# Five GpSimd DRAIN instructions among the last output scatters of a recurrence-and-experts kernel

## The chip, the core and the metric

The kernel runs on one core of one Trainium2 chip. The metric is device time in microseconds, from an execution's start to its end; several executions are timed and the median is taken. A separate, profiled execution left the page and the trace from which the rows below come. In those rows PE is TensorE (matmuls; PEld its weight loads), DVE is VectorE, ACT is ScalarE, POOL is GpSimd, SP is SyncE, and a small q behind a name (POOLq) means the engine's sequencer, which waits, branches and issues.

## What is computed

A gated recurrence over 4 sequences of 5056 steps, then a layer of 8 experts of which each token uses one. Cut to what matters:

```python
f = lower_bound + (1 - lower_bound) * sigmoid(f_logit)      # (4, 5056, 256)
h[t] = f[t] * h[t-1] + (1 - f[t]) * x[t]                    # per sequence; y[t] = h[t]
logits = y @ w_gate                                          # 20224 tokens, 8 experts
e = argmax(logits); p = softmax(logits)[e]
out[token] = p * (relu(y[token] @ w1[e]) @ w2[e])            # 256 -> 1024 -> 256
```

## The kernel before

**Units and buckets.** The 20224 tokens are cut into 79 units of 256. Each unit is gated, scanned, split into two fp16 halves and routed. Its rows are then written by GpSimd into a bucket of their expert in device memory: one indirect DMA of 128 rows at a time, the scatters to `buckets` (line 399, in `place`).

**Expert steps.** A step takes 256 rows of buckets (one tile of 256 or two of 128). `fetch` lets SP load them transposed into `xT` (line 531), with their gate weights and token numbers in `me` (line 533). `gemm1` makes the hidden layer in four pieces that ACT (line 567) and DVE (line 547) write into `hT`. `gemm2` multiplies `hT` with `w2s` on PE (lines 598 to 600), for the two halves of 128 tokens in turn. ACT scales each half into `ob` (line 604, three buffers in turn), and GpSimd writes it with an indirect DMA to the rows of `out` (line 605): the output scatters, two to a step. `step` runs `gemm1` of one step and `gemm2` of the step before it.

**Order.** In the main loop units run beside steps, their pieces placed by `fill`. PE, ACT and DVE keep the order in which the code is written; GpSimd and SP are ordered by the scheduler from the dependencies. GpSimd's queue holds nothing but scatters there: 158 to `buckets` and 162 to `out`. When the units are done, the loop at the end of the function runs what is left, with nothing beside it:

```python
    while todo or fetched:
        step(lambda k: None)
    while pend:
        gemm2(*factors(*pend.pop(0)), lambda k: None)
```

It makes 20 turns, and the last `gemm2` follows them: 21 pairs of output scatters in all, one pair to a turn and one behind. Up to three further tiles (`MAYBE`) are run behind a branch (lines 878 to 883) if the data asks for them; in this data it doesn't, and GpSimd then executes an `INC_SWDGE_SEM` instruction in the other arm (line 880), which sets the counts that the scatters of that arm would have set.

**The end.** At the close of the program (all of it recorded under line 967) SP waits for what is still open, every engine executes a DRAIN, a barrier joins them, GpSimd clears the semaphores, and a second barrier ends the program. GpSimd has one DRAIN at the start of the program too (line 963), and none between.

Of the kernel before, what the change touches and what calls it, by code (L numbers as in the profile page):

```python
# [45 lines left out]
INLINE = mybir.DependencyInfo(mybir.DependencyClass.NoSync, mybir.DependencyReason.SCHED_ONLY)  # L46
# [19 lines left out]
def moe_kernel(ctx: ExitStack, tc: tile.TileContext, x, fl, lb, wg, w1, w2, cst, tok, out, xb, S):  # L66
    nc = tc.nc
# [160 lines left out]
    scatters, based, pace = [], {}, []  # L228
# [3 lines left out]
    def inline(d, kind):  # L232

        for n in lined["O" if kind == "S" else "S"]:
            tc.add_manual_dep(d.ins, n, INLINE, reason="in the order of the row")
        lined["O" if kind == "S" else "S"].clear()
        lined[kind].append(d.ins.name)

    def free(d, *groups, keep=()):

        for k in groups:
            tc.declare_no_dep(d.ins, group=k, keep=[s.ins for s in keep], reason="different rows")
# [120 lines left out]
    def place(g, i0, ng, rows, m, sh, ex, oh, mx):  # L363
# [34 lines left out]
        def scatter(i):  # L398
            d = nc.gpsimd.indirect_dma_start(  # L399
                out=xb[:, :], out_offset=bass.IndirectOffsetOnAxis(ap=idx[:, i:i + 1], axis=0),  # L400
                in_=rows[:, i, 0:ROW], in_offset=None)
            free(d, "scatter", "load")
            if (i0 + ng) * P + P <= CAP:

                free(d, "blank")
            if pace:
                tc.add_manual_dep(d.ins, pace[0], PACED, reason="scatters apart")
            tc.add_to_no_dep_group("scatter", d.ins)
            inline(d, "S")
            scatters.append(d)  # L410
# [127 lines left out]
    def bases(t, tiles):  # L538

        if t not in based:  # L540
            based[t] = [nc.tensor.value_load(i[1], min_val=0, max_val=(E - 1) * WE) for _, i in tiles]
        return based[t]
# [6 lines left out]
    def gemm1(t, tiles, xT, me, n, fill):  # L549
        hT = p2.tile([P, 2, NF, UNIT], F16, tag="hT", name=f"hT{t}")  # L550
        evs = bases(t, tiles)
        for b in range(NF // 2):
            ps = pg1.tile([P, 2, UNIT], F32, tag="g1", name=f"g1_{t}_{b}")
            for q in range(2):
                f = 2 * b + q
                a = 0
                for ev, (nt, _) in zip(evs, tiles):
                    for c in range(2):
                        hi = w1s[:, ds(ev + (c * F + f * P), P)]
                        lo = w1s[:, ds(ev + (2 * F + c * F + f * P), P)]  # L560
                        o = ps[:, q, a:a + nt]
                        nc.tensor.matmul(o, lhsT=hi, rhs=xT[:, c, a:a + nt], start=c == 0, stop=False)  # L562
                        nc.tensor.matmul(o, lhsT=hi, rhs=xT[:, 2 + c, a:a + nt], start=False, stop=False)  # L563
                        nc.tensor.matmul(o, lhsT=lo, rhs=xT[:, c, a:a + nt], start=False, stop=c == 1)  # L564
                    a += nt
            hh = hT[:, 0, 2 * b:2 * b + 2, :n]
            pace[:] = [nc.scalar.activation(hh, ps[:, :, :n], AF.Relu).ins.name]  # L567
            behind()
            owed.append((hT[:, 1, 2 * b:2 * b + 2, :n], ps[:, :, :n], hh))
            drip(DRIP)  # L570
            fill(b)
        behind()
        return t, n, [ev for ev, (nt, _) in zip(evs, tiles) for _ in range(nt // P)], hT, me, tiles

    def factors(t, n, evs, hT, me, tiles):
        fac = sm.tile([P, 2], F32, tag="fac", name=f"fac{t}", bufs=3)
        ti, a = [], 0
        for nt, (_, _, ei, skip, _) in tiles:
            j = slice(a // P, (a + nt) // P)
            nc.scalar.activation(fac[:, j], me[:, j, 0], AF.Copy, scale=ei)  # L580
            to = me.bitcast(I32)[:, j, 1:2]
            if skip is not None:
                at = sm.tile([P, 1], I32, tag="ti", name=f"ti{t}_{a}", bufs=4)
                nc.vector.tensor_scalar(at, to[:, 0, :], skip, None, op0=ALU.add)
                to = at.unsqueeze(1)
            ti += [to[:, k, :] for k in range(nt // P)]
            a += nt
        return t, evs, hT, fac, ti

    def gemm2(t, evs, hT, fac, ti, fill):  # L590
        for j, ev in enumerate(evs):
            po = pg2.tile([P, 512], F32, tag="g2", name=f"g2_{t}_{j}")
            for f in range(NF):
                hi = w2s[:, ds(ev + f * D, D)]
                lo = w2s[:, ds(ev + (2 * F + f * D), D)]
                hh = hT[:, 0, f, j * P:(j + 1) * P]
                hl = hT[:, 1, f, j * P:(j + 1) * P]
                nc.tensor.matmul(po[:, :D], lhsT=hh, rhs=hi, start=f == 0, stop=False)  # L598
                nc.tensor.matmul(po[:, :D], lhsT=hh, rhs=lo, start=False, stop=False)  # L599
                nc.tensor.matmul(po[:, :D], lhsT=hl, rhs=hi, start=False, stop=f == NF - 1)  # L600
                if f == NF // 2 - 1:
                    fill(4 + 2 * j)
            ob = p2.tile([P, D], F32, tag="ob", name=f"ob{t}_{j}", bufs=3)
            pace[:] = [nc.scalar.activation(ob, po[:, :D], AF.Copy, scale=fac[:, j:j + 1]).ins.name]  # L604
            d = nc.gpsimd.indirect_dma_start(  # L605
                out=out[:, :], out_offset=bass.IndirectOffsetOnAxis(ap=ti[j], axis=0),
                in_=ob, in_offset=None, bounds_check=N - 1, oob_is_err=False)
            free(d, "out")
            tc.add_to_no_dep_group("out", d.ins)
            inline(d, "O")  # L610
            fill(5 + 2 * j)


    plan, n, taken = [], 0, 0
# [23 lines left out]
    todo, placing, drips, total, held = [], [], [], [], []  # L638
# [31 lines left out]
    def release(n=1):  # L670

        while n and held:
            held.pop(0)()
            n -= 1
# [47 lines left out]
    queue, fetched, pend, nst = [], [], [], 0  # L722

    def ready():
        return sum(t for t, _ in todo) + sum(f[4] for f in fetched)

    def prefetch():
        nonlocal nst
        while todo and len(fetched) < 3:
            tiles = [todo.pop(0)]  # L730
            if tiles[0][0] == P and todo and todo[0][0] == P:
                tiles.append(todo.pop(0))
            fetched.append(fetch(nst, tiles))
            nst += 1

    def step(fill, second=True):

        prefetch()
        if len(pend) > 1:
            gemm2(*factors(*pend.pop(0)), lambda k: None)  # L740
        last = factors(*pend.pop(0)) if pend and second else None
        pend.append(gemm1(*fetched.pop(0), fill))
        prefetch()

        def then(k):
            if k == 5 and fetched:
                bases(*fetched[0][:2])
            fill(k)
        if last:
            gemm2(*last, then)  # L750
        else:
            for k in range(4, 8):
                fill(k)
# [32 lines left out]
    for w in ORDER.split():  # L786
        k, n = w[0], int(w[1:] or 0)
# [53 lines left out]
    def fill(k):  # L841
        nonlocal here
        while coming and coming[0][0] <= here:
            coming.pop(0)[1]()
        here += 1
        short = ready() < SHORT
        if short or k in (1, 3) or k == 0 and len(held) > 4 or k == 5 and len(held) > 8:
            release(1 + short)
# [20 lines left out]
    spare = []  # L869
    while len(spare) < MAYBE and todo:  # L870
        spare.insert(0, todo.pop())
    while todo or fetched:
        step(lambda k: None)
    while pend:
        gemm2(*factors(*pend.pop(0)), lambda k: None)

    if spare:
        n = nc.values_load(total[0])
# [93 lines left out]
```

## Time and profile before

| | |
|---|---|
| median of 3 runs | 1018.64 us (1015.17 to 1020.44) |
| the profiled execution's own time | 1019.52 us |
| its span, first to last instruction | 1017.6 us |
| PE busy | 931.3 us (92%) |
| POOL busy | 330.2 us (32%), 326 instructions |
| mean granted TensorE clock | 0.987 of full |
| last matmul, last scatter, end | about 1004, 1005.6, 1017.6 us |

The page gives busy time by engine over the whole span. Waits, DRAINs and barriers are the sequencers' and not counted as busy there, so the closing sequence shows on the page only as an empty last slice; its instructions come out when the trace is asked for their line.

### The profile page before, as it was taken

The page shows a single profiled execution, that of the slowest core. Times are in us where ns is not written, and L with a number is a line of the kernel's source. Part 1 is how long each engine was busy: PE and PEld are TensorE (multiplying, and loading weights), DVE is VectorE, ACT ScalarE, POOL GpSimd, SP SyncE. Part 2 cuts the span into 40 slices and gives each one's busy share as a digit, 9 for nine tenths or more (in the row PEclk, how much of TensorE's full clock was granted, in tenths as well). Part 3 has the DMA queues.
Part 4 walks back from the last instruction along what each step waited for, and adds up shares of the span by engine and source line. Part 5 has one row for each costly group of instructions (what it writes and reads, how often), then busy time and mean ns, then how long its engine had stood idle before and what let it go on. Part 6 is the DMA issues. An engine that isn't in the chain of part 4 may idle for free.

```text
span 1017.6 us, 29588 instructions
## 1 busy us (share of the span) xinstructions
PE 931.3 (92%) x10971; PEld 850.5 (84%) x10971; DVE 656.9 (65%) x1816; ACT 499.4 (49%) x971; POOL 330.2 (32%) x326
## 2 busy tenths in 40 slices
PE   3538879999997999999999999999999999999994
PEld 2426779999986999998988999888888888899994
DVE  7898879887866787777878777676644322223220
ACT  4566545555555555555565555564433333333331
POOL 0151143433433334444443443334333111121111
PEclk9998999999999999999999999999999999999997
DMA  7997678778786887899998677775423222221210
GB/s 256 340 340 194 131 158 169 156 157 162 158 159 154 162 175 151 169 178 191 193 200 172 157 174 153 149 167 126 103 77 78 49 53 53 51 51 41 48 45 19
DMA packets 239774, 145.54 MB, mean 143 GB/s; under 512 B 205966, under 2 KB 207248, under 8 KB 237585
## 3 DMA queue, kind: packets, MB, share of 16 engines
q1 hardware_dynamic: 224272, 102.02, 47.5%
q0 software_dynamic: 15360, 41.60, 14.4%
q8 instruction: 94, 1.54, 0.7%
q14 instruction: 48, 0.39, 0.1%
HBM read 58.57 MB, written 43.16 MB: 100 GB/s over the span
## 4 chain that ended last, share of the span: by engine, by line
PE 72%; DVE 10%; DMA 8%; issue 3%; ACT 3%; SPq 2%; POOL 1%; POOLq 0%; ACTq 0%; DVEq 0%
PE g L562 12%; PE g L564 12%; PE g L563 12%; PE g L598 11%; PE g L599 11%; PE g L600 11%; DMA w2s<-in_w 3%; DMA ft<-in_f 3%; DVE xt L305 2%; DMA xT<-buckets 2%; DVE hT L547 2%; DVE ft L330 1%; PE wps L178 1%; PE tp L339 1%; SPq L531 1%
## 5 line engine op out<-in xcount | busy, mean ns | idle before, releaser
L562 PE MATMUL g<-xT,w1s 128*128 128x128 f16 (+1 forms) x1968 | 401.7, 237 | 11.5 <-DMA xT<-buckets 5.5
L564 PE MATMUL g<-xT,w1s 128*128 128x128 f16 (+1 forms) x1968 | 401.8, 237 | 0.0
L563 PE MATMUL g<-xT,w1s 128*128 128x128 f16 (+1 forms) x1968 | 401.8, 237 | 0.0
L598 PE MATMUL g<-w2s,hT 128*128 x1296 | 353.5, 273 | 3.8 <-DVE am L308 2.1
L600 PE MATMUL g<-w2s,hT 128*128 x1296 | 353.5, 273 | 0.0
L599 PE MATMUL g<-w2s,hT 128*128 x1296 | 353.4, 273 | 0.0
L547 DVE SCALAR_TENSOR_TENSOR hT<-g,hT 128x512 f16<-128x512 f32 x324 | 220.4, 686 | 205.0 <-ACT hT L567 202.8
L567 ACT ACTIVATE hT<-g 128x512 f16<-128x512 f32 x324 | 190.8, 593 | 128.9 <-PE g L564 123.3
L605 POOL DMA_INDIRECT out_dram<-ob,me x142 | 143.7, 1012 | 333.9 <-ACT ob L604 258.4
L399 POOL DMA_INDIRECT buckets<-rows,idx x158 | 166.3, 1053 | 259.6 <-ACT hT L567 162.5
L563 PEld LDWEIGHTS <-w1s 128*128 x1968 | 193.5, 98 | 17.5 <-issue 10.4
L562 PEld LDWEIGHTS <-w1s 128*128 x1968 | 193.4, 98 | 10.3 <-DMA xT<-buckets 1.5
L564 PEld LDWEIGHTS <-w1s 128*128 x1968 | 193.5, 98 | 7.1
L604 ACT ACTIVATE ob<-g,fac 128x256 f32<-128x256 f32 x162 | 76.3, 471 | 197.3 <-PE g L600 189.4
L599 PEld LDWEIGHTS <-hT 128*128 128x128 f16 x1296 | 126.8, 98 | 16.6 <-issue 2.9
L598 PEld LDWEIGHTS <-hT 128*128 128x128 f16 x1296 | 126.8, 98 | 16.4 <-issue 2.5
L600 PEld LDWEIGHTS <-hT 128*128 128x128 f16 x1296 | 126.8, 98 | 14.9
L305 DVE TENSOR_TENSOR_SCAN xt<-ft,xt,xt 128x256 f32<-128x256 f32 (+2 forms) x156 | 110.7, 728 | 0.0
L278 ACT ACTIVATE ft<-ft,fa,fs 128x256 f32<-128x256 f32 x158 | 91.1, 591 | 0.8
L330 DVE SCALAR_TENSOR_TENSOR ft<-xt,m,ft 128x256 f16<-128x256 f32 x158 | 72.6, 480 | 28.9 <-ACT ft L323 24.5
L323 ACT ACTIVATE ft<-xt,m 128x512 f16<-128x512 f32 x79 | 57.0, 721 | 69.5 <-DVE m L320 67.8
L274 ACT ACTIVATE ft<-ft 128x512 f32<-128x512 f32 x79 | 49.2, 622 | 64.7 <-DMA ft<-in_f 54.5
(128 smaller groups left out, 609.9 us busy)
## 6 DMA issues: line engine op xcount, KB each, us to landing
ft<-in_f SPq DMA_DIRECT2D x79, 256.0 KB
xt<-in_x SPq DMA_DIRECT2D x79, 256.0 KB
w2s<-in_w SPq DMA_DIRECT2D x14, 1024.0 KB
rows<-ft SPq DMA_TRANSPOSE x158
buckets<-rows,idx POOLq DMA_INDIRECT x158
out_dram<-ob,me POOLq DMA_INDIRECT x142
ws<-in_w SPq DMA_DIRECT2D x2, 1024.0 KB
xT<-buckets SPq DMA_TRANSPOSE x126
```

The source lines that it names most:

```text
L278: nc.scalar.activation(ft[:, c, :], ft[:, c, :], AF.Identity, scale=fs[:, c:c + 1], bias=fa[:, c:c + 1])
L305: nc.vector.tensor_tensor_scan(xt[:, c, a:b], ft[:, c, a:b], xt[:, c, a:b], ini, op0=ALU.mult, op1=ALU.subtract)
L399: d = nc.gpsimd.indirect_dma_start(out=xb[:, :], out_offset=bass.IndirectOffsetOnAxis(ap=idx[:, i:i + 1], axis=0), in_=rows[:, i, 0:ROW], ...
L547: nc.vector.scalar_tensor_tensor(lo, ps, 0.0, hh, op0=ALU.max, op1=ALU.subtract)
L562: nc.tensor.matmul(o, lhsT=hi, rhs=xT[:, c, a:a + nt], start=c == 0, stop=False)
L563: nc.tensor.matmul(o, lhsT=hi, rhs=xT[:, 2 + c, a:a + nt], start=False, stop=False)
L564: nc.tensor.matmul(o, lhsT=lo, rhs=xT[:, c, a:a + nt], start=False, stop=c == 1)
L567: pace[:] = [nc.scalar.activation(hh, ps[:, :, :n], AF.Relu).ins.name]
L598: nc.tensor.matmul(po[:, :D], lhsT=hh, rhs=hi, start=f == 0, stop=False)
L599: nc.tensor.matmul(po[:, :D], lhsT=hh, rhs=lo, start=False, stop=False)
L600: nc.tensor.matmul(po[:, :D], lhsT=hl, rhs=hi, start=False, stop=f == NF - 1)
L605: d = nc.gpsimd.indirect_dma_start(out=out[:, :], out_offset=bass.IndirectOffsetOnAxis(ap=ti[j], axis=0), in_=ob, in_offset=None, bounds_c ...
```

## The change

`settle` issues a DRAIN on GpSimd. It has no wait and sets no semaphore. Two dependencies that hold for the scheduler alone (`INLINE`) put it behind the last output scatter that was issued before it and ahead of the next one. The last loop calls it after its turns 0, 6, 12 and 18, and after the turn that leaves no tile to fetch and two fetched, which is turn 17: five in all, four of them by the count of six. In the built program they stand behind the second scatter of steps 60, 66, 72, 77 and 78; step 80 is the last. Nothing else is added, removed or moved: the rows of every engine stand in the same order as before.

```diff
+    settled, outs = [], []
+
+    def settle():
+
+        d = nc.gpsimd.drain()
+        for n in outs:
+            tc.add_manual_dep(d.ins, n, INLINE, reason="behind the scatters")
+        settled.append(d.ins.name)
+
...
             free(d, "out")
             tc.add_to_no_dep_group("out", d.ins)
             inline(d, "O")
+            for n in settled:
+                tc.add_manual_dep(d.ins, n, INLINE, reason="behind the drain")
+            settled.clear()
+            outs[:] = [d.ins.name]
             fill(5 + 2 * j)
...
+    turn = 0
     while todo or fetched:
         step(lambda k: None)
+        if turn % 6 == 0 or not todo and len(fetched) == 2:
+            settle()
+        turn += 1
```

## Rows read from the trace of the kernel before

**Rows 1.** Busy time by stretch; columns are engines, then granted clock, DMA share, GB/s.
```profile
790.00:998.60 208.60, 208.60 (x2382) 192.55 (x2380) 57.47 (x100) 70.82 (x146) 37.97 (x39) 1.00 0.20 48
998.60:1005.61 7.01, 5.21 (x48) 4.41 (x46) 0.00 (x0) 1.79 (x5) 2.91 (x3) 1.00 0.14 44
1005.61:1017.60 11.99, 0.00 (x0) 0.00 (x0) 0.00 (x0) 0.00 (x0) 0.00 (x1) 0.57 0.02 5
```

**Rows 2.** Closing line 967: count, duration min/median/max in ns, first and last start.
```profile
L967 POOLq DRAIN  x3: 40/107/8885, 1007.9 to 1017.3; - x3
L967 SPq DRAIN  x3: 7/7/7, 1008.5 to 1017.0; - x3
L967 DVEq DRAIN  x2: 10/14/17, 995.2 to 1017.1; - x2
L967 ACTq DRAIN  x2: 8/8/8, 1004.7 to 1017.0; - x2
L967 PEldq DRAIN  x2: 8/8/8, 1006.5 to 1017.1; - x2
```

**Rows 3.** The same line on POOL between 1007 and 1010 us alone.
```profile
L967 POOLq DRAIN  x1: 8885/8885/8885, 1007.9 to 1007.9; - x1
```

**Rows 4.** DMA between 1006.9 and 1016.8 us: packets, and the only queue with any.
```profile
DMA packets 1, 0.02 MB, mean 2 GB/s; under 512 B 0, under 2 KB 0, under 8 KB 0
...
q8 instruction: 1, 0.02, 0.6%
```

**Rows 5.** POOL's instructions of line 963, at the program's start, in ns.
```profile
L963 POOLq INC_SWDGE_SEM  x1: 31/31/31, 0.2 to 0.2; - x1
...
L963 POOLq DRAIN  x1: 189/189/189, 0.4 to 0.4; - x1
```

**Rows 6.** POOL's groups of scatters over the span: count, busy us, mean ns, idle before.
```profile
L399 POOL DMA_INDIRECT buckets<-rows,idx x158 | 166.3, 1053 | 259.6 <-ACT hT L567 162.5 <-DVE wm L188 45.5 <-DVE idx L396 31.1
L605 POOL DMA_INDIRECT out_dram<-ob,me x142 | 143.7, 1012 | 333.9 <-ACT ob L604 258.4 <-ACT fac L580 41.7 <-DMA rows<-ft 8.5
L605 POOL DMA_INDIRECT out_dram<-ob,ti x20 | 19.5, 973 | 81.2 <-ACT ob L604 64.8 <-ACT fac L580 14.8 <-ACTq L880 1.6
```

**Rows 7.** Line 880 on POOL, the arm in which the extra tiles are skipped.
```profile
L880 POOLq INC_SWDGE_SEM  x1: 2330/2330/2330, 1005.5 to 1005.5; - x1
```

**Rows 8.** POOL's timeline: start, duration, instruction, idle before it and its releaser.
```profile
758.55 0.97 POOL L399 DMA_INDIRECT buckets<-rows,idx  x1 [0.45 <-ACT hT L567]
759.86 0.96 POOL L399 DMA_INDIRECT buckets<-rows,idx  x1 [0.34 <-ACT hT L567]
...
796.47 0.97 POOL L605 DMA_INDIRECT out_dram<-ob,me  x1 [6.93 <-ACT ob L604]
799.03 0.97 POOL L605 DMA_INDIRECT out_dram<-ob,me  x1 [1.60 <-ACT fac L580]
806.95 0.97 POOL L605 DMA_INDIRECT out_dram<-ob,me  x1 [6.94 <-ACT ob L604]
809.51 0.97 POOL L605 DMA_INDIRECT out_dram<-ob,me  x1 [1.60 <-ACT fac L580]
...
861.91 0.97 POOL L605 DMA_INDIRECT out_dram<-ob,me  x1 [1.60 <-ACT fac L580]
...
988.80 0.97 POOL L605 DMA_INDIRECT out_dram<-ob,ti  x1 [1.65 <-ACT fac L580]
996.78 0.97 POOL L605 DMA_INDIRECT out_dram<-ob,ti  x1 [7.01 <-ACT ob L604]
...
1004.64 0.97 POOL L605 DMA_INDIRECT out_dram<-ob,ti  x1 [1.65 <-ACTq L880]
```

**Rows 9.** SP's waits before its `me` loads, line 533, between 862 and 866 us.
```profile
L533 SPq EVENT_SEMAPHORE  x2: 17/22/28, 864.3 to 864.4; - x2
```

**Rows 10.** SP's own waits between 796 and 860 us: total, times, longest, in us.
```profile
SPq L533 <- DMA out_dram<-ob,me: 33.7, 5, 8.2
SPq L531 <- PE g L564: 5.5, 5, 1.3
```

**Rows 11.** ACT's timeline: the second scaling into `ob` behind step 61.
```profile
819.25 0.47 ACT L604 ACTIVATE ob<-g,fac 128x256 f32<-128x256 f32 x1 [2.10 <-PE g L600]
```

## The prediction

> **What bounds the kernel now.** I read the busy time by stretch first. From 790 to 998.6 us, where the change puts its DRAINs, PE is busy for all of the 208.60 us at full granted clock (2.4 GHz) and POOL for 37.97 us [rows 1]. So in that stretch only PE's own work counts, and POOL is covered unless it makes PE wait. The last scatter ends at 1005.61 us. Then come 11.99 us, 1.2% of the span, in which no engine is busy [rows 1]. The chain on the page stops at that last scatter and says nothing of this tail, so I asked for the line of the closing sequence. There one instruction stands out: of POOL's three DRAINs one took 8885 ns, and it is the one that starts at 1007.9 us [rows 2, 3]. SP, DVE, ACT and PE need 7 to 17 ns for theirs, and SP, the last of these four, starts its own at 1008.5 us [rows 2]. Everybody is ready by then but POOL, which drains until 1007.9 + 8.9 = 1016.8 us. From there the barriers take 1017.6 - 1016.8 = 0.8 us. About 8.2 us of the span are thus nothing but this one DRAIN.
>
> **What the long DRAIN does.** It isn't waiting for a transfer: between 1006.9 and 1016.8 us the DMA engines moved one packet, of instructions, and none of the scatters' [rows 4]. It isn't the fixed price of a DRAIN on POOL either: the DRAIN at the program's start took 189 ns, behind four memsets and no scatter [rows 5], and the two that follow the long one, with nothing issued between, took 107 and 40 ns [rows 2]. What lies between the short one at 0.4 us and the long one is 158 + 142 + 20 = 320 scatters and no other DRAIN [rows 6]. I read it as work that every scatter leaves behind on POOL and that a DRAIN clears, spread over all 320 at 8885 / 320 = 28 ns each, or over fewer recent ones at more each, if part of it is cleared on the way. The trace can't tell these two apart, and the sum hardly depends on it.
>
> One page of the Trainium skill speaks against the change: "VectorE: DVE Perf Modes", section "The DRAIN you can't avoid", puts the DRAINs of a program's preamble and postamble at a constant of about 12 ns on all five engines. ACT, SP and PE agree (7 to 8 ns in rows 2), POOL's 8885 ns does not. By that figure five DRAINs would cost 0.06 us, and there would be nothing at the end to save.
>
> **The change, part by part.**
>
> *The last DRAIN.* With the change the fifth added DRAIN stands behind the scatter that starts at 988.80 us; after it come 4 scatters (996.78 to 1004.64 us) and then the end [rows 8]. At 28 ns each the final DRAIN has 0.1 us of work. If only the last 40 scatters count, at 8885 / 40 = 222 ns each, it has 0.9 us. The bounds from the rows are 0.04 us (the shortest on POOL) and 8.9 us (nothing cleared). I take 0.1 to 0.9 us, for the DRAIN behind few or no scatters is what rows 2 and 5 show to be cheap. It starts at 1007.9 us as now and is over by 1008.0 to 1008.8 us. What is late next is SP's closing waits, done at 1008.5 us. So the barriers begin at about 1008.6 us and the end comes at 1008.6 + 0.8 = 1009.4 us: a gain of 1017.6 - 1009.4 = 8.2 us, and at the 0.9 us end of the price some 0.2 us less.
>
> *The instruction ahead of it.* `INC_SWDGE_SEM` on line 880 took 2330 ns from 1005.5 to 1007.9 us [rows 7], and SP's closing waits follow it. At the start of the program, before any scatter, an instruction of the same name took 31 ns [rows 5]. If it too pays for what the scatters left behind, it shrinks with 4 of them in place of 320. Bounds: 0 and 2.3 us. Only a part of that shows. The next thing late is the last scatter's landing: a scatter started at 861.91 us released SP at 864.3 us [rows 8, 9], 2.4 us later, so the one at 1004.64 us lands at about 1007.1 us instead of the 1007.9 us from which SP goes on now. That is 0.8 us more, the whole gain then 9.0 us. I take 0.8 us, since four scatters behind a DRAIN are nearer to the program's start than to 320 of them; 0 stays as the other end.
>
> *The added DRAINs, and what covers them.* Each stands behind the second scatter of a pair, and POOL is then idle until ACT has the next output: 6.94 us in the pair that ends at 799.03 + 0.97 = 800.0 us [rows 8]. The first DRAIN has 280 scatters behind it (158 and 61 pairs): 280 x 28 = 7.8 us, or 8.9 us if all the work lies in recent ones. It ends between 807.8 and 808.9 us, where the next scatter is due at 806.95 us. With about 0.2 us to start, that scatter comes 1 to 2.2 us late. The one behind it is due at 809.51 us; scatters have followed each other by 1.31 us [rows 8], so it comes 0 to 1 us late, and the next pair is on time. The others have 12, 12, 10 and 2 scatters behind them: 0.3 us or less at 28 ns each, 2.7 us at 222 ns, plus the wait for a scatter that is still landing (2.4 us from its start). All lie inside the 6.9 us.
>
> Who waits behind that first, late pair? SP, which takes the landing of an output scatter as the sign to reload `me` and then `xT`. It waits for it five times between 796 and 860 us, and for PE behind that up to 1.3 us [rows 10], so a second scatter that is 1 us late mostly disappears in the wait for PE. And ACT, whose third `ob` from there reuses the buffer at 819.25 us [rows 11]: the late scatter lands by 809.2 + 2.4 = 811.6 us, 7.6 us early. PE waits for neither. I put this part at 0. Without that cover it would be 8 to 9 us for the first DRAIN, all that the end gives back.
>
> **The sum.** 8.2 + 0.8 + 0 = 9.0 us, from 1019.52 us of the profiled execution to 1010.5 us. The runs' median is 0.9 us below the profiled one (1018.64 us), so I forecast 1018.64 - 9.0, about 1009.8 us with a little of the upper bounds in it. Its own range, from a gain of 8 to 9 us and runs that lie 3 us below and 2 us above their median, is 1006 to 1014 us.
>
> **The rivals.**
>
> *Nothing is cleared: the last DRAIN has a price of its own.* It could be that the first DRAIN behind any scatter costs 8.9 us, however many there are. For it: no row of before shows a DRAIN behind a few scatters, only behind none and behind 320. Against it: what it would do for 8.9 us with no packet moving [rows 4] is hard to name. Then all five take 8.9 us, delay the next pair as worked out above without touching PE, and the end stays: 1018.6 us, no change. "PSUM — Partial Sum Buffer", section "Engine vs sequencer instructions", of the Trainium skill says that a drain waits for the engine to go fully idle; with a wait alone the final one would behave like this rival, and rows 4 show no transfer for it to wait on. 10%.
>
> *Slower: a DRAIN that outlasts its cover.* In the middle of the run SP's loads and DRAIN share the machine, and the work might go slower than in the silent tail. The point from which that decides is ACT's `ob` at 819.25 us: a scatter has to be started by 819.25 - 2.4 = 816.8 us, so a DRAIN from 800.0 us may take 16.6 us at most. At twice its measured price, 17.8 us, each of the DRAINs would hold ACT, and PE behind it, by 1.2 us, and if the fixed price of the first rival held too, all five would: 1018.6 + 5 x 1.2 = 1024.6 us. It needs both a doubling and a price that doesn't fall. 4%.
>
> *The change doesn't do what it says.* A DRAIN without a wait could be passed by the scatter behind it, or stand elsewhere in POOL's queue. The dependencies fix its place on both sides, and the tail shows POOL's DRAIN holding back the barrier. This would look like the first rival, and is counted there.
>
> *Half of it.* The work left behind could belong mostly to the latest scatters, the four after the last DRAIN paying some 1 us each: a final DRAIN of 4 us, a gain of about 4.5 us, 1014 us. 3%.
>
> **How the numbers follow.** Forecast 83%, fixed price 10%, half 3%, slower 4%. A measurement of this kernel can tell about 0.5%, 5 us, from no change. Of the 83% nearly all, 81%, end below 1013.5 us; "half" and the fixed price fall within 0.5%, with a little of the forecast's upper end: 15%; slower 4%. The range of the forecast alone, 1006 to 1014 us, holds 80% with the rest outside, so it is the range.
>
> **What would show it.** In the profile after: POOL's first DRAIN of line 967 at under 1 us instead of 8885 ns, and the span's end about 4 us behind the last scatter's start instead of 13; the first added DRAIN near 8 us at 800 us, the next four far shorter; the scatter due at 806.95 us late by 1 to 2 us, and PE as busy as before up to 998 us; `INC_SWDGE_SEM` on its line below 2330 ns. I am wrong if the first added DRAIN is short while the last is still near 8.9 us (then it isn't cleared work), if all are near 8.9 us (a fixed price), or if PE has gaps behind 800 us.

## The result, and the profile after

The changed kernel takes 1007.72 us, the median of 6 runs (1006.71 to 1009.83), against 1017.4 us for the kernel before over 6 runs (1013.78 to 1020.44). The ratio is 0.9909, with a 95% interval of 0.9886 to 0.9932: faster by 0.9%, some 9.3 us. The median of before wanders by several us from one series of runs to the next (1017.4 us here, 1014.24 and 1013.71 us on the two chips of the experiments), so the ratios to runs of before on the same chip are what counts below.

The stretches of the changed kernel, to be held against [rows 1] (columns as there):

```profile
790.00:996.50 206.50, 206.50 (x2363) 190.65 (x2362) 57.03 (x99) 70.30 (x146) 37.63 (x39) 1.00 0.20 48
996.50:1004.68 8.18, 6.37 (x59) 5.46 (x56) 0.00 (x0) 1.79 (x5) 3.24 (x4) 1.00 0.16 52
1004.68:1007.80 3.12, 0.00 (x0) 0.00 (x0) 0.00 (x0) 0.00 (x0) 0.00 (x0) 0.96 0.07 20
```

PE is busy without a gap beside the five DRAINs, as it was. The stretch in which no engine is busy has shrunk from 11.99 to 3.12 us, and that is 8.9 us of the gain. The profiled spans differ by 9.8 us (1017.6 and 1007.8); the other 0.9 us arose before the first added DRAIN (the scatter ahead of it started at 799.03 us before and at 798.10 us now), in code that the change doesn't touch.

The closing sequence of the changed kernel (now line 984; the skipped arm is line 897), by line: count, duration min/median/max in ns, first and last start. It answers [rows 2] and [rows 7]:

```profile
L984 POOLq DRAIN  x3: 46/107/1641, 1004.9 to 1007.5; - x3
L984 SPq DRAIN  x3: 7/7/7, 1006.9 to 1007.2; - x3
...
L897 POOLq INC_SWDGE_SEM  x1: 248/248/248, 1004.6 to 1004.6; - x1
```

The closing DRAIN of POOL takes 1641 ns instead of 8885 and is over at 1006.5 us. SP's first comes at 1006.9 us, so POOL no longer ends last. `INC_SWDGE_SEM` fell with it, from 2330 to 248 ns.

The five added DRAINs, each by its own stretch, in the same columns, and POOL's timeline around the first and at the end (start, duration, instruction, idle before it and its releaser):

```profile
L243 POOLq DRAIN  x1: 6835/6835/6835, 797.9 to 797.9; - x1
L243 POOLq DRAIN  x1: 3180/3180/3180, 860.7 to 860.7; - x1
L243 POOLq DRAIN  x1: 3212/3212/3212, 924.0 to 924.0; - x1
L243 POOLq DRAIN  x1: 3115/3115/3115, 977.0 to 977.0; - x1
L243 POOLq DRAIN  x1: 2769/2769/2769, 987.6 to 987.6; - x1
```

```profile
795.53 0.97 POOL L614 DMA_INDIRECT out_dram<-ob,me  x1 [6.93 <-ACT ob L613]
798.10 0.97 POOL L614 DMA_INDIRECT out_dram<-ob,me  x1 [1.59 <-ACT fac L589]
806.01 0.97 POOL L614 DMA_INDIRECT out_dram<-ob,me  x1 [6.94 <-DMA me<-buckets]
...
1003.70 0.97 POOL L614 DMA_INDIRECT out_dram<-ob,ti  x1 [1.65 <-ACTq L897]
```

The record of such a DRAIN starts 0.2 us ahead of the scatter that it stands behind. The first is over at 797.9 + 6.8 = 804.7 us, and the next pair starts at 806.01 us, 10.48 us behind 795.53 us, the spacing that it had in [rows 8]. Nothing was late at all.

### The profile page after: what moved, and what is told of

Same layout as the page of the kernel before. It is cut to its first block, busy times and chain, and to the rows that moved or that the text cites. A ratio compares the mean times of both kernels' runs of the same rounds, so it can differ in the third digit from the quotient of the medians.

```text
span 1007.8 us, 29593 instructions
## 1 busy us (share of the span) xinstructions
PE 931.2 (92%) x10971; PEld 850.3 (84%) x10971; DVE 657.2 (65%) x1816; ACT 501.0 (50%) x971; POOL 330.6 (33%) x326
## 4 chain that ended last, share of the span: by engine, by line
PE 78%; DVE 8%; DMA 6%; ACT 3%; issue 2%; SPq 2%; POOL 0%; POOLq 0%; ACTq 0%; DVEq 0%
PE g L607 13%; PE g L571 13%; PE g L608 12%; PE g L609 12%; PE g L572 12%; PE g L573 12%; DMA ft<-in_f 2%; DMA w2s<-in_w 2%; DMA xT<-buckets 2%; DVE xt L314 1%; PE tp L348 1%; PE wps L178 1%; DVE hT L556 1%; DVE ft L339 1%; DVE xt L292 1%
## 5 line engine op out<-in xcount | busy, mean ns | idle before, releaser
L572 PEld LDWEIGHTS <-w1s 128*128 x1968 | 193.4, 98 | 19.1 <-issue 12.1
L607 PEld LDWEIGHTS <-hT 128*128 128x128 f16 x1296 | 127.1, 98 | 16.6 <-issue 2.5
```

## The experiments

All are set against runs of the kernel before on the same chip. A scatter is called open as long as the next DRAIN still has to pay for it, and let go when no DRAIN has to any more. Each profile is of one execution. For the tail I use the time from the last scatter's start to the end of the span: 1017.6 - 1004.64 = 13.0 us before, 1007.8 - 1003.70 = 4.1 us now.

### Only the first DRAIN

```diff
-        if turn % 6 == 0 or not todo and len(fetched) == 2:
+        if turn == 0:
```

> Only the first added DRAIN, behind step 60, with 280 scatters behind it; 40 scatters follow it and meet the closing DRAIN alone. Theory A, the work is spread over all scatters since the last DRAIN (24 to 28 ns each): the closing DRAIN has 1.0 to 1.1 us of work, hidden beside the last landing, and the gain over before is 9 us as with five. Theory B, only some 100 to 130 scatters are ever open and each costs 55 to 90 ns: the closing DRAIN needs 2.2 to 3.6 us, of which 1 to 2 us show, and the gain is 7 to 8 us. Rival, a fixed price behind any scatter: the closing DRAIN is 6.8 to 8.9 us again and the time is that of before.

Measured: a ratio of 0.9885 (0.985 to 0.992). Its closing sequence:

```profile
L984 POOLq DRAIN  x3: 46/107/3321, 997.8 to 1001.7; - x3
...
L897 POOLq INC_SWDGE_SEM  x1: 968/968/968, 996.8 to 996.8; - x1
```

With 40 scatters behind the added DRAIN the closing one takes 3321 ns: 82 ns each (with some 50 ns of its own, see below), inside theory B's range and three times theory A's price. The tail is 1002.0 - 995.9 = 6.1 us, 2 us more than with all five. So the later DRAINs are worth about 2 us of tail. The runs don't show that: their ratio is even a little lower than with five (0.9909), and the intervals are too wide for 2 us.

### Only the DRAIN behind step 77

```diff
-        if turn % 6 == 0 or not todo and len(fetched) == 2:
+        if not todo and len(fetched) == 2:
```

> Only the added DRAIN behind step 77, with 314 scatters behind it and 6 after it. Theory A: it needs 314 x 24.4 = 7.7 us. Theory B: the same 6.8 us as the one with 280 behind it, for the open scatters are as many. Both: it ends before the next scatter is due (8.0 us after the scatter ahead of it), the closing DRAIN is as short as with five, and the gain over before is 9 us, so the other four are not needed. Rival, a fixed price: no gain.

Measured: a ratio of 0.9915 (0.9891 to 0.994), the same gain as five. The DRAIN, and POOL's timeline around it:

```profile
L243 POOLq DRAIN  x1: 9612/9612/9612, 972.0 to 972.0; - x1
```

```profile
972.23 0.97 POOL L614 DMA_INDIRECT out_dram<-ob,ti  x1 [1.65 <-ACT fac L589]
982.50 0.97 POOL L614 DMA_INDIRECT out_dram<-ob,ti  x1 [9.29 <-issue]
983.78 0.98 POOL L614 DMA_INDIRECT out_dram<-ob,ti  x1 [0.30 <-issue]
```

Both theories missed its length. From the end of the scatter ahead of it (973.2 us) it worked for 8.4 us, against 5.6 us for the same DRAIN behind 280 scatters (798.10 + 0.97 to 804.7 us): 34 scatters more cost 2.8 us more, 82 ns each. So neither all scatters count alike (8.4 us / 314 = 27 ns, but the next 34 cost three times that), nor is there a constant number of open ones. It also outlasted its cover: the next scatter was due 7.98 us behind the last, at 980.21 us, and came 2.3 us late. That cost nothing that can be told: PE had no gap there, as the stretch below shows, and the tail is 1003.0 - 998.67 = 4.3 us.

```profile
960.00:995.00 35.00, 35.00 (x464) 33.06 (x462) 9.02 (x18) 11.96 (x27) 6.82 (x7) 1.00 0.14 40
```

### One DRAIN with its cover gone

```diff
-        if turn % 6 == 0 or not todo and len(fetched) == 2:
-            settle()
...
     while pend:
-        gemm2(*factors(*pend.pop(0)), lambda k: None)
+        gemm2(*factors(*pend.pop(0)), lambda k: settle() if k == 5 else None)
```

> One DRAIN only, between the last two scatters, where POOL is idle for 1.65 us: the same work, with most of its cover gone. A and B: 6.8 to 8.7 us long from about 1001.7 us; the last scatter starts at 1008.7 to 1010.6 instead of 1004.6 us, the tail behind it is the short one, and the end is 4 to 6 us later than with the DRAIN under cover, 3 to 5 us earlier than before (the transfers' landing and SP's closing waits, which before ran beside the long DRAIN, now stand behind it). Rival, the work is done beside whatever follows and blocks nothing: the last scatter is on time and the gain is 9 us.

Measured: a ratio of 0.9984 (0.996 to 1.0008), no gain that can be told. POOL's timeline and the DRAIN:

```profile
989.79 0.97 POOL L614 DMA_INDIRECT out_dram<-ob,ti  x1 [1.65 <-ACT ob L613]
1000.47 0.97 POOL L614 DMA_INDIRECT out_dram<-ob,ti  x1 [9.70 <-issue]
```

```profile
L243 POOLq DRAIN  x1: 10022/10022/10022, 989.6 to 989.6; - x1
```

The last scatter was due 2.62 us behind 989.79 us, at 992.41 us, and started at 1000.47 us, 8.1 us late. The tail behind it is the short one (4.1 us). From the due time the end is 12.1 us away, against 13.0 us before. I had expected a scatter 4 to 6 us late and a gain of 3 to 5 us: I had let the DRAIN start 1.3 us too early, at its record's start instead of the end of the scatter ahead of it, and had its work too small. I had also put the scatter 0.2 us behind the DRAIN's end; it came 0.9 us behind (989.6 + 10.0 = 999.6 us, then 1000.47 us). The reading stands: what the change gives is the cover, not less work.

### What one scatter costs a DRAIN

```diff
+        if late:
+            tc.add_manual_dep(d.ins, pace[0], PACED, reason="when all has landed")
...
-        step(lambda k: None)
-        if turn % 6 == 0 or not todo and len(fetched) == 2:
-            settle()
+        step(lambda k: settle(True) if k == 3 and turn in (1, 2, 4, 7, 11, 16) else None)
```

`pace[0]` names ACT's latest piece of the hidden layer when `settle` is called, here the fourth; the DRAIN waits for it.

> Six DRAINs in the last loop, each made to wait until ACT has the fourth piece of the hidden layer, some 6 us behind the last scatter, so that everything has landed and the DRAIN's length is its work alone. Scatters behind them: 282, 2, 4, 6, 8 and 10. Theory A at 24 to 28 ns: 6.9 to 7.9 us, then 0.05, 0.10, 0.15, 0.20, 0.25 us above a base. Theory B at 55 to 90 ns: the first 6.8 to 8.9 us, the rest 0.11 to 0.18 us up to 0.55 to 0.9 us. If the 2.8 to 3.2 us that the DRAINs 2 to 5 took in the changed kernel were work and not waiting for a landing, the small ones stay near 3 us. The first one starts at 804 us, ends near 811 us and holds two scatters back by 2 to 4 us; PE should not notice (limit worked out before: a scatter may start at 816.8 us). Gain 8 to 9 us.

Measured: a ratio of 0.9891 (0.9852 to 0.993). The six DRAINs, each by its own stretch:

```profile
L243 POOLq DRAIN  x1: 5618/5618/5618, 803.7 to 803.7; - x1
L243 POOLq DRAIN  x1: 211/211/211, 814.2 to 814.2; - x1
L243 POOLq DRAIN  x1: 364/364/364, 835.2 to 835.2; - x1
L243 POOLq DRAIN  x1: 527/527/527, 866.6 to 866.6; - x1
L243 POOLq DRAIN  x1: 691/691/691, 908.8 to 908.8; - x1
L243 POOLq DRAIN  x1: 854/854/854, 961.8 to 961.8; - x1
```

Behind 2, 4, 6, 8 and 10 scatters they take 211 to 854 ns: a straight line of (854 - 211) / 8 = 80 ns a scatter on a base of 50 ns. This is theory B's price. It also shows that the 2.8 to 3.2 us of the small DRAINs in the changed kernel are waiting: with everything landed the one behind 2 scatters needs 211 ns, beside 2769 ns where it stood right behind them (some 1.2 us of which passed before the end of the scatter ahead of it). Behind 280 scatters waiting for the landing adds nothing: 5.6 us here, and 5.6 us from the scatter's end in the changed kernel. The first one (280 scatters, not the 282 of the expectation) takes 5618 ns, which by the line is (5618 - 50) / 80.4 = 69 open scatters. By the same line the closing DRAIN of before had (8885 - 50) / 80.4 = 110.

It was also late for the next pair, as meant. Timeline and stretch:

```profile
810.24 0.97 POOL L616 DMA_INDIRECT out_dram<-ob,me  x1 [10.66 <-ACT hT L578]
811.52 0.97 POOL L616 DMA_INDIRECT out_dram<-ob,me  x1 [0.30 <-issue]
817.00 0.97 POOL L616 DMA_INDIRECT out_dram<-ob,me  x1 [4.51 <-ACT ob L615]
```

```profile
795.00:860.00 65.00, 65.00 (x598) 58.26 (x597) 16.60 (x24) 21.59 (x43) 12.63 (x13) 1.00 0.23 54
```

The pair started 3.7 and 2.4 us late against the 10.48 us spacing, the one behind it on time, and PE was busy for all of the 65.00 us.

### A DRAIN behind every step

```diff
         if last:
             gemm2(*last, then)
         else:
             for k in range(4, 8):
                 fill(k)
+        if outs:
+            settle()
```

The condition in the last loop is taken out; with the line above, `step` itself calls `settle`, in the main loop too.

> A DRAIN behind every step, 80 in all, 60 of them in the main loop beside the units, where POOL's idle stretches are shorter and the scatters to the buckets follow. Theory: with 2 to 10 scatters open each is 0.2 to 0.9 us of work or a wait of some 1.5 us for the last landing, POOL has room for it (busy 251 of 640 us between 100 and 740 us), the units and PE don't notice, the closing DRAIN is the short one: gain over before 9 us, as with five. Rival that ends slower than the changed kernel: the DRAINs hold back scatters to the buckets, the loads of buckets come later and PE waits; at 1 us for each step that is 60 us, the time then far above before.

Measured: a ratio of 0.9926 (0.9907 to 0.9944), within the interval of the changed kernel. By line, and the main loop's stretches:

```profile
L243 POOLq DRAIN  x80: 2716/3678/7949, 114.8 to 990.1; - x80
```

```profile
100.00:400.00 300.00, 283.63 (x4015) 266.31 (x4015) 244.49 (x728) 166.16 (x351) 110.03 (x109) 0.99 0.75 161
400.00:740.00 340.00, 339.47 (x3678) 307.83 (x3677) 251.21 (x686) 189.34 (x375) 142.35 (x139) 1.00 0.73 162
```

The same stretches of before:

```profile
100.00:400.00 300.00, 279.99 (x3952) 262.18 (x3950) 239.68 (x717) 164.43 (x347) 110.33 (x107) 0.98 0.76 158
400.00:740.00 340.00, 338.24 (x3691) 307.22 (x3689) 253.85 (x690) 189.15 (x376) 141.29 (x139) 1.00 0.77 164
```

Eighty DRAINs, 60 of them beside the units, cost nothing that can be told and gain no more than five. PE's busy time in the main loop's two stretches is 283.6 and 339.5 us, against 280.0 and 338.2 us before: it waits no more than it did. The first DRAIN has 18 scatters behind it and the others have 2 to 6, by the curve 1.5 us of work and 0.2 to 0.5 us; the rest of the 2.7 to 7.9 us is waiting, for the scatter ahead to start and to land. The rival, buckets arriving late for PE, is out. One part of the expectation was missed, the short closing DRAIN:

```profile
L984 POOLq DRAIN  x3: 46/113/3279, 996.4 to 1000.7; - x3
L984 SPq DRAIN  x3: 7/7/7, 1000.1 to 1000.4; - x3
```

Behind 2 open scatters 3279 ns are a wait, not work. The last scatter started at 995.83 us, and SP's first closing DRAIN, behind its wait for the landings, came 4.3 us later, against 3.2 us with five. So the last landing took longer in this execution, and the tail is 1001.0 - 995.83 = 5.2 us. Why it did stays open.

### Where the open scatters go

The curve left one thing unexplained: 69 open of 280, 110 of 320. Two kernels put one DRAIN into the main loop and a second one behind step 60 that waits until all has landed.

```diff
+        if outs and pend[-1][0] == 17:      # 38 in the other kernel
+            settle()
...
+        step(lambda k: settle(True) if k == 3 and turn == 1 else None)
```

> Two DRAINs: one in the main loop behind 88 scatters, one behind 280 that waits until all has landed. From the lengths so far a DRAIN costs 0.05 us + 0.080 us for each open scatter, and 69, 104, 109 and 110 were open behind 280, 314, 319 and 320. Theory S (they pile up to a limit of some 105 to 113 and are then let go at once): 88 open at the first, 7.1 us; then 192 more with one letting-go between, 79 to 87 open, 6.4 to 7.0 us. Theory D (they were let go once, at a certain point of the program near the 211th): 7.1 us, then 5.6 us as without the first. Theory W (only recent ones count, a window): 5.6 us or less at both.

> The same with the first DRAIN behind 185 scatters. Theory S: 72 to 80 open, 5.8 to 6.5 us, then 95 more, all open, 7.7 us. Theory D: 185 open, 14.9 us, then 5.6 us. Theory W: 5.6 us at both.

Measured, each DRAIN by its own stretch and the scatter ahead of the first one, for the kernel with 88 and then for the one with 185 scatters ahead of the first DRAIN (one execution each):

```profile
308.70 0.99 POOL L616 DMA_INDIRECT out_dram<-ob,me  x1 [0.30 <-ACT fac L591]
L243 POOLq DRAIN  x1: 8923/8923/8923, 308.0 to 308.0; - x1
L243 POOLq DRAIN  x1: 7077/7077/7077, 799.1 to 799.1; - x1
```

```profile
545.24 1.02 POOL L616 DMA_INDIRECT out_dram<-ob,me  x1 [1.63 <-ACT ob L615]
L243 POOLq DRAIN  x1: 7782/7782/7782, 545.0 to 545.0; - x1
L243 POOLq DRAIN  x1: 7812/7812/7812, 797.8 to 797.8; - x1
```

A DRAIN right behind a scatter is counted from that scatter's end: 308.70 + 0.99 to 308.02 + 8.92 us (the row's 308.0 is 308.02 us in the trace), 7.3 us, and 545.24 + 1.02 to 545.00 + 7.78 us, 6.5 us. By the line that is 90 and 80 open; the second DRAINs, 7077 and 7812 ns, are 87 and 97 open. The first kernel's 88 were all still open. The second's 185 were not, about 105 had gone. Of the 192 that followed in the first kernel 105 had gone; of the 95 that followed in the second, none. In the kernel before 280 - 69 = 211, twice 105, had gone. So they pile up and go in lots of about 105, as theory S has it; the four lengths are within 0.2 us of its ranges. Theory D (185 open, 14.9 us) and theory W (5.6 us each time) are out. Within a lot nothing goes one by one, or the 95 would have shrunk. The letting go itself is read off the lengths and no row shows it: from the 105th to the 280th scatter of the kernel before, among which two lots went, POOL's longest idle time is 6.9 us and its longest scatter 1.5 us, while a DRAIN would pay 105 x 0.08 = 8.4 us for a lot. What sets the lot wasn't tried. It doesn't go at 105, since the last stretch of before reached 110 open without letting go; a fixed count above 110 at which 105 go would fit all the lengths.

## Why the prediction was right, and where it was not

I forecast 1009.8 us, a gain of 9.0 us, from a DRAIN that clears work before the end instead of at it. The measured gain is 9.3 us by the runs and 8.9 us by the tail of the profiles. Of the 2.1 us between 1009.8 and 1007.72 us, 1.2 us is the median of before, 1018.64 us over three runs and 1017.4 us over six.

*The last DRAIN.* The 8.2 us came as worked out: POOL's closing DRAIN fell below what SP needs anyway. Its work, 0.1 to 0.9 us forecast, is 0.05 + 4 x 0.08 = 0.4 us by the curve; the 1641 ns on record, above the 1 us that I had named as a sign of being right, are mostly the wait for the last landing, which I hadn't counted and which SP waits for too.

*`INC_SWDGE_SEM`.* I took the 0.8 us on the guess that it pays for the same backlog. It does: 183, 248, 288, 374, 968 and 2330 ns with 1, 4, 6, 10, 40 and 110 open (the kernel with the DRAIN in the last gap, the changed one, the one with step 77 alone, the paced one, the one with the first DRAIN alone, and before), a line of 20 ns each. The three that aren't shown above:

```profile
L895 POOLq INC_SWDGE_SEM  x1: 183/183/183, 1001.4 to 1001.4; - x1
L897 POOLq INC_SWDGE_SEM  x1: 288/288/288, 999.6 to 999.6; - x1
L897 POOLq INC_SWDGE_SEM  x1: 374/374/374, 1005.1 to 1005.1; - x1
```

It shrank, and the last scatter's landing became the next thing late, as the working said. From the last scatter's start to SP's first closing DRAIN it was 1008.5 - 1004.64 = 3.9 us before and is 1006.9 - 1003.70 = 3.2 us now: 0.7 of the 0.8 us. The other 8.2 of the 8.9 us are the DRAIN's.

*The first DRAIN.* This step was mis-sized. I gave it 7.8 to 8.9 us and made the next scatter 1 to 2.2 us late. It needed 5.6 us behind the scatter's end, and nothing was late. Of the two readings that I allowed, all 320 scatters at 28 ns was wrong. Fewer at more each was right in kind, 110 at 80 ns, but I took as many to be open behind 280 as behind 320; how many are open depends on how far the current lot has filled, and it was 69. That the first DRAIN fitted into its cover was luck of that kind: behind step 77 it had some 104 to clear and outlasted it. "About 0.2 us to start" for the scatter behind a late DRAIN was too little as well: it took 0.9 us three times (981.6 to 982.50 us, 999.6 to 1000.47 us, and 803.7 + 5.6 = 809.3 to 810.24 us). None of this moved the sum, since the cover analysis held with room to spare: scatters 2.3 to 3.7 us late (step 77 alone, and the paced DRAINs) left PE without a gap.

*Cover.* "Without that cover it would be 8 to 9 us" was borne out: 8.1 us in the last gap, and the gain gone.

*The rivals.* A fixed price is refuted by five DRAINs of different lengths and by the curve. "Half of it" needed 1 us for each of the latest scatters; it is 80 ns. The slower one needed a doubled price beside traffic; in the main loop the DRAIN behind 88 scatters worked 7.3 us, 82 ns each, the same price as in the silent tail. Its threshold of 16.6 us was never reached, so the price beyond it stays untested.

## What to carry to other kernels

Look at what an execution does after its last useful instruction: here no engine was busy for 12 us, the page's chain ended ahead of it, and one row of the closing line named the cause. Where GpSimd issues many indirect DMAs, look at how long its closing DRAIN takes; if it is long, put a DRAIN a few DMAs before the end, into a stretch where GpSimd idles longer than the backlog needs or where nobody waits for it, and leave only a handful behind it. Here one was enough; put where GpSimd idled for 1.65 us and the end waited for it, it gained nothing.

## What the runs showed of the hardware that I had not expected

- A DRAIN on GpSimd behind indirect DMAs (all of 128 rows here) costs 50 ns and 80 ns for each that hasn't been let go, long after it landed. The open ones go in lots of about 105, or at a DRAIN. Whether the price goes by the DMA or by its rows wasn't tried.
- It also waits for transfers: behind two scatters it took 2769 ns while they were landing and 211 ns when they had landed. "PSUM — Partial Sum Buffer", section "Engine vs sequencer instructions", of the Trainium skill says that a drain waits for the engine to go fully idle. The trace agrees, if landing and the unreleased backlog are counted to the engine.
- `INC_SWDGE_SEM` pays for the same backlog, some 20 ns for each open DMA on a base of 160 to 180 ns; at the program's start, before any, it took 31 ns [rows 5].
- The scatter behind a DRAIN that outlasted its cover started 0.9 us behind the DRAIN's end, three times.
